# Loads and transposes of the first batches re-ordered in a fused attention and star-ReLU MLP kernel

## The chip, the cores and the metric

The kernel runs on one core of a Trainium2 chip. The metric is the device time of one execution in microseconds. Five engines work side by side: TensorE (PE, with its weight loads shown apart as PEld), VectorE (DVE), ScalarE (ACT), GpSimd (POOL) and SyncE (SP). Each follows its own list of instructions, and they wait for each other by semaphores. Transfers are issued from the queues of SP, ACT and POOL.

## The reference

`x` is (8, 8, 512, 64): batch, head, token, width. `state` is (8, 8, 32, 64). `w_in` is 512 x 2048 and `w_out` 2048 x 512.

```python
scores = scale * x @ state^T                     # 512 x 32 per batch and head
xread = softmax(scores) @ state
sread = softmax(scale * state @ x^T) @ x         # 32 x 64 per batch and head
X = concat([xread, sread], axis=tokens)          # heads side by side: 4352 rows of 512
h = X @ w_in
g = s * relu(h) ** 2 + b
out = g @ w_out
```

## The kernel before, in words

**Order.** The work is declared as operations with an engine (or a choice of ACT and DVE), a key, inputs, outputs, buffers and a duration. A planner (`Plan.order`, L28) runs through a model of time of its own and writes down, for each engine, one fixed order: of the operations that its model takes for ready, the one with the smallest key comes next. For PE it inserts filler matmuls (`filler`, L1094, tile `warm`) early on. The keys are offsets in a table `K` (L283). On the chip each engine then runs its list strictly as written, so an operation whose input is late holds all that stands behind it.

**Stages for one batch.** `x[b]` comes to SBUF in fp16 as `xn`. `xT` is its transpose, `stT` that of the state. `T` = scores (PE), `E` = exp (ACT), `D` = sums of `E` over a head's 32 slots (PE, with the block matrix `bones16`), `R` = exp(-ln D) (ACT, two steps, L559 and L566), `a4` = `E` * `R` (DVE). The state is multiplied into `w_in` first: `M` = state @ w_in, four chunks per batch with two halves each (`Mps` on PE, then a cast on ACT or DVE, L310 or L312). Then `h` = `M` against `a4` for 16 blocks `f`, `relu` (L779 on ACT, L771 on DVE), and a square on DVE (L785) gives `g`. The product with `w_out` accumulates in two PSUM banks `o`. Batch 0 uses plain row blocks. The later batches use a seven-product scheme with sums `u` of the weights and `pd` of `g` (DVE). For the second read of the softmax, `a2` (DVE) is transposed by SP as `aT`, `V` is `aT` @ `xn` (PE), and the collected state rows are run through the same MLP at the end (`h_sr`, `osr`). A column sum of `w_out` (`wsum_ps`, L903) makes the bias; `s` and `b` are applied when `o` is read.

**Loads before.** ACT's queue brings the identity, the first state part and `bones16`; SP's queue brings `x[0]` in four fp32 parts `xf` (L248), which ACT casts. All else goes through POOL's queue, which casts to fp16 on the way, in the order of `SEQ` (L404):

```python
SEQ = "wi0 x1 wi1 stf1 wo0 wi2 wo1 wi3 wo2 wo3 x2 sb x3 x4 x5"
```

Here `wi0` to `wi3` are the parts of `w_in`, `wo0` to `wo3` those of `w_out`, `stf1` the state of batches 1 and 2, and `sb` the two scalars `s` and `b`; `stf1` and `sb` are issued on SP behind a small POOL instruction. The last state part, `stf2`, waits for `wo3`. Batches 0 to 2 are transposed on PE (`xT_mm` into PSUM tile `xTps`, `xT_copy` on DVE); batches 3 to 7 by SP's DMA transposes (`dma_xT`, L462), their state by one more (`stTd`). `NB_HW = 3` sets this limit.

Of the kernel before, what the change touches and what calls it, by code (L numbers as in the profile page):

```python
# [13 lines left out]
class Plan:  # L14
# [13 lines left out]
    def order(self, filler, fill_until, ready):  # L28
# [25 lines left out]
        mode, channel, log, now, done_n = False, 7.0, [], 0.0, 0  # L54
        times = []

# [15 lines left out]
        while done_n < len(ops):  # L72
            for e in free_at:
# [29 lines left out]
                if best is None:  # L103
                    fill = 0.43 if now < 7.0 else 0.22
                    if e == "PE" and now < fill_until and not any(since[i] < now + fill for i in cand[e]):
                        free_at[e] = now + fill
                        times.append(free_at[e])
                        log.append((now, len(log), "PE", filler, "warm", free_at[e]))
                    continue
# [13 lines left out]
                if land is not None:  # L123
                    kind, span = land
                    if kind == "load":
                        done = max(channel, end + 2.0) + span
                        channel = max(channel, done)
                    elif kind == "tp" and now < channel - 4.0:
                        end, done = now + 4.0, now + 9.0
                    else:  # L130
                        done = end + span
# [25 lines left out]
def kernel(  # L157
# [66 lines left out]
    nc.vector.memset(warm, 0.0)  # L224
    ident16 = konst.tile([P, P], FP16, name="ident16")
    ident_dr = nc.inline_tensor(np.eye(P, dtype=np.float16), name="ident_const")
    bones_np = np.kron(np.eye(4), np.ones((Ns, Ns))).astype(np.float16)
    bones16 = konst.tile([P, P], FP16, name="bones16")
    bones_dr = nc.inline_tensor(bones_np, name="bones_const")
    st_v = state.rearrange("b (g hf) j d -> (hf j) (b g) d", g=NG)  # L230
    NB_HW = 3
    stf = konst.tile([P, NG, D], FP32, name="stf")
    stf1 = konst.tile([P, (NB_HW - 1) * NG, D], FP32, name="stf1")
    stf2 = konst.tile([P, (B - NB_HW) * NG, D], FP32, name="stf2")
    xf = [upool.tile([P, H // 2, SCH * D], FP32, name=f"xf_{i}", tag="u") for i in range(2)]
    x0_v = x[0].rearrange("h (q c) d -> q h (c d)", q=P)

    def xf_part(i):
        return xf[i // 2][:, 2 * (i % 2) : 2 * (i % 2) + 2]
# [6 lines left out]
    nc.scalar.dma_start(stf, st_v[:, 0:NG, :])  # L246
    for i in range(4):
        nc.sync.dma_start(xf_part(i), xf_heads(x0_v, i))  # L248
    nc.scalar.dma_start(bones16, bones_dr.ap())
# [5 lines left out]
    s_bc = konst.tile([P, 1], FP32, name="s_bc")  # L255
    b_bc = konst.tile([P, 1], FP32, name="b_bc")
# [6 lines left out]
    st16 = konst.tile([P, B * NG, 2, D], FP16, name="st16")  # L263
    xn = {}
    xn[0] = xpool.tile([P, H, SCH, D], FP16, name="xn_0", tag="xn")

    def cast_x0(eng, i):
        eng(
            xf_heads(xn[0], i).rearrange("p h c d -> p h (c d)"),
            xf_part(i),  # L270
        )

    def cast_st(eng, src, n0, n):
        for k in range(2):
            eng.tensor_copy(st16[:, n0 : n0 + n, k, :], src)

    def late_dma(dst, src):


        nc.gpsimd.memset(dst, 0.0)  # L280
        nc.sync.dma_start(dst, src)

    K = dict(  # L283
        h1=4.4, hs=0.6, M0=-5.6, M1=0.9, T1=0.0, x2=24.6, T2=23.7, D2=27.2, M2=35.3, V0=27.7, V1=21.3, u=12.3,
        us=5.1, pd1=12.5, o0=13.1, o2=23.0, w=26.2, r=0.5, T=-9.8, D=3.1, Mb=6.4, V=8.6, S=3.6, S0=0.1, E=-0.5,
        L=-6.2, a4=-4.7, Mc=1.5, pd=13.4, solo=2.0, hsr=-4.1, Ssr=0.0,
# [3 lines left out]
    stTd = konst.tile([P, (B - NB_HW) * NG, P], FP16, name="stTd")  # L290
# [43 lines left out]
    def cast_x0(i):  # L334
        def fn(e):
            copy_on(
                e,
                xf_heads(xn[0], i).rearrange("p h c d -> p h (c d)"),
                xf_part(i),
# [4 lines left out]
    def cast_st(e, src, n0, n):  # L344
        for k in range(2):
            copy_on(e, st16[:, n0 : n0 + n, k, :], src)

    add(DV(0.4), -30, lambda e: cast_st(e, stf, 0, NG), ["stf"], [("st", 0)])
    for i in range(4):
        add(  # L350
            (DV(0.35), AC(0.5)),
            -29 + i,
            cast_x0(i),
            [("xf", i)],
            [("x", 0, i)],
            [("u", f"xf{i // 2}"), ("xn", "x0")],
        )


    def load(key, dur, span, fn, makes, bufs=(), after=0.0):  # L360
        add(("POOL", dur), key, fn, [], makes, bufs, ("load", span), after=after)
# [21 lines left out]
    def load_x(b, h0=0, h1=H):  # L383
        def fn(e):
            if h0 == 0:
# [8 lines left out]
    def late(dst, src):  # L394
        def fn(e):
            nc.gpsimd.memset(dst, 0.0)
# [4 lines left out]
    gate = konst.tile([P, 2], FP16, name="gate")  # L401
    nc.gpsimd.tensor_copy(gate, ident16[:, 0:2])
    SEQ = "wi0 x1 wi1 stf1 wo0 wi2 wo1 wi3 wo2 wo3 x2 sb x3 x4 x5"
    seq = [(t,) if t in ("stf1", "sb") else (t[:-1], int(t[-1])) for t in SEQ.split()]  # L404
    for n, it in enumerate(seq):
        key = -40 + n
        if it[0] == "wi":
            load(key, 0.8, 4.2 if it[1] == 0 else 2.8, load_wi(it[1]), [it], after=3.4)
        elif it[0] == "wo":
            load(key, 0.8, 2.8, load_wo(it[1]), [it], after=3.4)  # L410
        elif it[0] == "x":
            b = it[1]
            load(
                key, 0.9, 2.9 if b == 1 else 3.9, load_x(b),
                [("x", b, i) for i in range(4)], [("xn", f"x{b}")], after=3.4,
            )
        elif it[0] == "stf1":
            load(key, 0.3, -3.0, late(stf1, st_v[:, NG : NB_HW * NG, :]), [it], after=3.4)
        else:
            load(key, 0.15, 0.1, late(s_bc, moe_s.to_broadcast((P, 1))), [("s",)], after=3.4)  # L420
            load(key + 0.1, 0.15, 0.1, late(b_bc, moe_b.to_broadcast((P, 1))), [("b",)], after=3.4)

    def load_stf2(e):
        nc.gpsimd.tensor_copy(stf2[:, 0, 0:2], wo[3][:, 0, 0:2])
        nc.sync.dma_start(stf2, st_v[:, NB_HW * NG :, :])

    add(("POOL", 0.3), -21, load_stf2, [("wo", 3)], [("stf2",)], (), ("side", 4.0))
    n1 = (NB_HW - 1) * NG
    add(
        DV(0.4), 0, lambda e: cast_st(e, stf1, NG, n1),  # L430
        [("stf1",)], [("st", 1), ("st", 2)],
    )
    add(
        ("POOL", 1.7), -19, lambda e: cast_st(e, stf2, NB_HW * NG, (B - NB_HW) * NG),
        [("stf2",)], [("st", 3)],
    )
# [8 lines left out]
    def dma_stT(e):  # L445
        nc.sync.dma_start_transpose(
            stTd, st16[:, NB_HW * NG :].rearrange("p n k d -> p (n k d)")
        )

    add(("SP", 1.5), 18, dma_stT, [("st", 3)], [("stT", b) for b in range(NB_HW, B)], land=("tp", 3.0))  # L450

    def xT_of(b, h):
        if b < NB_HW:
# [3 lines left out]
    def dma_xT(b, i):  # L457
        def fn(e):
            if "xT" not in A[b]:
                A[b]["xT"] = apool.tile([P, H, 2, P], FP16, name=f"xT_{b}", tag="xT")  # L460
                A[b]["stT"] = stTd[:, (b - NB_HW) * NG : (b - NB_HW + 1) * NG]
# [7 lines left out]
    def stT_mm(b):  # L469
        def fn(e):  # L470
            A[b]["stTps"] = att_ps([P, NG, P], FP16, f"stTps_{b}")
            for g in range(NG):
                mm(
                    A[b]["stTps"][:, g, :],
                    st16[:, b * NG + g].rearrange("p k d -> p (k d)"),
# [6 lines left out]
    def stT_copy(b):  # L482
# [647 lines left out]
```

The softmax here doesn't subtract the row's maximum and nothing guards it: scores larger than these inputs give would overflow.

## Time and profile before

| what | value |
|---|---|
| median of 4 runs | 213.67 us (213.44 to 214.24) |
| the profiled execution's own time | 213.55 us |
| its span in the profile | 211.4 us |
| PE busy | 204.1 us, 97% |
| DVE busy | 175.3 us, 83% |
| ACT busy | 132.7 us, 63% |
| PE groups of the `o` products | 123 us in all |
| filler matmuls (`o<-warm`) | 24, 8.2 us |
| PE share of the chain that ended last | 90% |

The profile shows one execution. Busy shares are averages over the whole span, while the change touches almost only the first 45 us, so the table says which engine carries the kernel but not what the change is worth. The filler matmuls count as busy PE although they compute nothing that is kept. Ends of matmuls are modelled, and a group of matmuls in a timeline row can overlap the row behind it by some tenths of a microsecond.

### The profile page before, as it was taken

Reading aid. Unit: us, or ns where it says so; the run is one execution under the profiler, and the core shown is the slowest. Engines: PE = TensorE matmul, PEld = TensorE weight load, DVE = VectorE, ACT = ScalarE, POOL = GpSimd, SP = SyncE. Lnnn points to the kernel's source line nnn. Section 1 sums busy time; section 2 is a strip of 40 time slices with the busy share of each in tenths; the row PEclk is TensorE's granted clock in tenths of the full one; section 3 lists DMA queues with packets and bytes.
Section 4 is the critical chain, followed back from the end, with each engine's and each line's share of the span. In section 5 each row is a group of like instructions: output and inputs, shape, how many; then the busy total and the mean of one; then the engine's idle time right before and its main releaser. Section 6 shows DMA issues by size and latency. Waiting matters only on the chain.

```text
span 211.4 us, 4963 instructions
## 1 busy us (share of the span) xinstructions
PE 204.1 (97%) x1976; PEld 132.4 (63%) x1976; DVE 175.3 (83%) x412; ACT 132.7 (63%) x288; POOL 37.0 (17%) x60
## 2 busy tenths in 40 slices
PE   5998999999999999999999999999999999999993
PEld 2542333544557676667766776677676777888882
DVE  1268999999988869999988998899989988697652
ACT  4569997696375965796478657974697444632200
POOL 4833100040125261012101200111111111110000
PEclk9999999999999999999999999999999999999998
DMA  6999999999578994553064211321142111211142
GB/s 203 163 197 202 190 205 198 183 144 233 116 151 140 155 254 81 118 77 116 26 125 109 79 50 53 67 89 54 50 59 99 53 50 39 70 50 50 36 143 74
DMA packets 41463, 24.05 MB, mean 114 GB/s; under 512 B 25824, under 2 KB 39648, under 8 KB 41440
## 3 DMA queue, kind: packets, MB, share of 16 engines
q0 software_dynamic: 13840, 15.21, 36.6%
q1 hardware_dynamic: 27040, 8.40, 23.3%
q8 instruction: 15, 0.25, 0.5%
q10 hardware_dynamic: 560, 0.13, 0.3%
q14 instruction: 8, 0.07, 0.1%
HBM read 17.37 MB, written 8.91 MB: 124 GB/s over the span
## 4 chain that ended last, share of the span: by engine, by line
PE 90%; ACT 6%; DMA 2%; issue 0%; DVE 0%; SPq 0%
PE o L209 49%; PE h L209 25%; PE Mps L209 4%; PE h_sr L209 3%; PE osr L209 3%; ACT g L779 2%; PE xTps L209 2%; DMA xf<-in_x_dram 2%; PE D L209 2%; ACT M L310 1%; PE V L209 1%; ACT E L540 1%; PE T L209 1%; ACT D L559 1%; ACT R L566 1%
## 5 line engine op out<-in xcount | busy, mean ns | idle before, releaser
L779 ACT ACTIVATE g<-h 128x512 f16<-128x512 f32 x126 | 73.4, 601 | 41.5 <-PE h L209 41.3
L209 PE MATMUL h<-a,M 128*128 128x512 f16 x256 | 73.8, 379 | 0.6 <-ACT g L779 0.5
L785 DVE TENSOR_TENSOR g<-g 128x512 f16<-128x512 f16 x128 | 52.7, 420 | 3.7 <-ACT g L779 2.2
L209 PEld LDWEIGHTS <-pd 128*128 128x128 f16 x448 | 42.6, 98 | 20.1 <-issue 3.4
L209 PEld LDWEIGHTS <-g 128*128 128x128 f16 x400 | 39.1, 98 | 19.4 <-issue 0.2
L209 PE MATMUL o<-u,pd 128*128 128x256 f16 x336 | 45.9, 273 | 0.0
L209 PE MATMUL o<-wo,g 128*128 128x256 f16 (+1 forms) x288 | 45.5, 296 | 0.0
L1036 POOL DMA_DIRECT2D out_dram<-c x24 | 16.3, 679 | 103.8 <-DVE c L1024 101.0
L209 PEld LDWEIGHTS <-M 128*128 128x128 f16 x256 | 24.1, 98 | 13.2 <-issue 4.6
L310 ACT CAST M<-Mps 128x512 f16<-128x512 f32 x45 | 25.3, 595 | 7.1 <-PE Mps L209 7.1
L1024 DVE SCALAR_TENSOR_TENSOR c<-o,s_bc,bias_bc 128x512 f32<-128x512 f32 x28 | 21.0, 750 | 7.3 <-PE o L209 6.6
L801 DVE TENSOR_TENSOR pd<-g 128x1024 f16<-128x1024 f16 x28 | 19.2, 686 | 0.3
L1024 DVE SCALAR_TENSOR_TENSOR c<-o,s_bc,c 128x512 f32<-128x512 f32 x21 | 15.7, 750 | 1.9 <-PE o L209 1.6
L209 PE MATMUL o<-wo,pd 128*128 128x256 f16 x112 | 16.2, 273 | 0.0
L209 PE MATMUL o<-u,g 128*128 128x256 f16 x112 | 15.5, 273 | 0.0
L312 DVE CAST M<-Mps 128x512 f16<-128x512 f32 x19 | 13.0, 687 | 2.0 <-PE Mps L209 1.9
L773 ACT ACTIVATE g_sr<-h_sr 128x256 f16<-128x256 f32 x16 | 6.1, 383 | 10.5 <-PE h_sr L209 10.4
L540 ACT ACTIVATE E<-T 128x256 f16<-128x256 f32 x32 | 11.8, 389 | 1.1 <-PE T L209 1.1
L812 DVE TENSOR_TENSOR pd<-g,pd 128x512 f16<-128x512 f16 x28 | 11.8, 421 | 0.4
L387 POOL DMA_DIRECT2D xn<-in_x_dram x13 | 10.4, 818 | 8.1 <-DMA wi<-in_moe_w_in_dram 3.7
L810 DVE TENSOR_TENSOR pd<-g,pd 128x512 f16<-128x512 f16 x28 | 11.7, 418 | 0.0
L559 ACT ACTIVATE D<-D 128x512 f32<-128x512 f32 x16 | 9.6, 601 | 1.6 <-PE D L209 1.4
(71 smaller groups left out, 162.8 us busy)
## 6 DMA issues: line engine op xcount, KB each, us to landing
out_dram<-c POOLq DMA_DIRECT2D x24, 256.0 KB, 2.5
xn<-in_x_dram POOLq DMA_DIRECT2D x5, 512.0 KB, 21.9
wi<-in_moe_w_in_dram POOLq DMA_DIRECT2D x4, 512.0 KB, 14.3
wo<-in_moe_w_out_dram POOLq DMA_DIRECT2D x4, 512.0 KB, 19.8
xf<-in_x_dram SPq DMA_DIRECT2D x4, 256.0 KB, 3.7
out_dram<-osb POOLq DMA_DIRECT2D x4, 256.0 KB, 4.4
xn<-in_x_dram POOLq DMA_DIRECT2D x8, 128.0 KB, 4.2
out_dram<-c SPq DMA_DIRECT2D x4, 256.0 KB, 2.5
```

Of the source, the lines that this page charges most:

```text
L209: return nc.tensor.matmul(out, lhsT, rhs, start=start, stop=stop, tile_position=tp, is_transpose=is_transpose, skip_group_check=True,)
L310: nc.scalar.copy(dst, src)
L312: ENG[e].tensor_copy(dst, src)
L540: nc.scalar.activation(a["E"][g][:, 256 * m : 256 * m + 256], a["T"][m][:, g, :], AF.Exp, scale=scale, accum_out=a["rs"][:, g, m : m + 1],)
L559: nc.scalar.activation(A[b][f"D{g}"], A[b][f"D{g}"], AF.Ln)
L779: nc.scalar.activation(g_of(name, f), OSB["h", name, f], AF.Relu)
L785: ENG[e].tensor_mul(g_of(name, f), g_of(name, f), g_of(name, f))
L801: nc.vector.tensor_tensor(pd[:, :, 0:2], g4[:, :, 1:2, :].to_broadcast((P, 2, 2, t)), g4[:, :, 0:4:3, :], ALU.subtract,)
L810: nc.vector.tensor_tensor(pd[:, :, 2], g4[:, :, 3], pd[:, :, 0], ALU.subtract)
L812: nc.vector.tensor_tensor(pd[:, :, 3], g4[:, :, 2], pd[:, :, 2], ALU.subtract)
L1024: nc.vector.scalar_tensor_tensor(t, src, s_bc, add, ALU.mult, ALU.add)
L1036: ENG[e].dma_start(dst[:, rows:SCH:2, hD * h : hD * h + hD], SN[b, name])
```

## The change

- The order of POOL's loads becomes `wi0` at once, then `wi1 wi2 wo0 wo1 wi3 wo2 wo3 x2 x3 x4 x5`. `x[1]` leaves this list: SP brings it in four fp32 parts, as `x[0]` before, each behind a small POOL copy that waits until the third part of `x[0]` has landed; eight casts instead of four follow. POOL's queue goes on with `wi1` when the first part of `x[1]` has landed.
- State comes as two parts of 128 KB, for batches 0 and 1 at the start and for batches 2 and 3 behind `wo1`, with contiguous rows of 1 KB, and one part of 256 KB for batches 4 to 7 behind `wo3`. PE transposes the first two parts (four matmuls each); `stT_copy` now sorts the columns.
- Batch 2 joins the batches that SP transposes (`NB_T = 2`).
- `s` and `b` come behind `wo2`, to four partitions each, and are spread by a DVE copy and a DVE transpose.
- `x[3]` waits on POOL for `aT` of batch 1.
- `bones16` is made by DVE memsets instead of a transfer.
- `xT_copy` of batch 0 is split in halves, one of which may go to ACT. The `relu` of the state rows becomes two instructions.
- The planner: nine fillers at the start, other durations for loads and transposes, other keys, DVE allowed for `relu` of every batch.

```diff
+        for k in range(9):
+            log.append((free_at["PE"], len(log), "PE", filler, "warm", free_at["PE"] + 0.43))
+            free_at["PE"] += 0.43
...
-                    fill = 0.43 if now < 7.0 else 0.22
+                    fill = 0.22
...
+    nc.vector.memset(bones16, 0.0)
+    for q in range(4):
+        nc.vector.memset(bones16[Ns * q : Ns * q + Ns, Ns * q : Ns * q + Ns], 1.0)
+    st_v = state.rearrange("(t b) h (j r) d -> (b h j) t r d", b=2, r=4)
+    st_w = state[4:B].rearrange("b (g hf) j d -> (hf j) (b g) d", g=NG)
+    stf = konst.tile([P, 2, 4, D], FP32, name="stf")
+    stf2 = konst.tile([P, 8, D], FP32, name="stf2")
...
-    nc.scalar.dma_start(stf, st_v[:, 0:NG, :])
+    nc.scalar.dma_start(stf[:, 0], st_v[:, 0])
...
-    nc.scalar.dma_start(bones16, bones_dr.ap())
...
+            AC(0.5) if n < 3 else (DV(0.35), AC(0.5)),
+            -29 + n if b == 0 else K["xc"] + 0.1 * i,
+            cast_x(b, i),
...
+            if b == 3:
+                nc.gpsimd.tensor_copy(gate, A[1]["aT"][:, :, 0, 0])
...
-    SEQ = "wi0 x1 wi1 stf1 wo0 wi2 wo1 wi3 wo2 wo3 x2 sb x3 x4 x5"
+    SEQ = "wi1 wi2 wo0 wo1 wi3 wo2 wo3 x2 x3 x4 x5"
...
+    def load_first(e):
+        load_wi(0)(e)
+        for i in range(4):
+            nc.gpsimd.tensor_copy(xf_part(1, i)[:, 0, 0:2], xf_part(0, 2)[:, 0, 0:2])
+            nc.sync.dma_start(xf_part(1, i), xf_heads(x_v[1], i))
+        nc.gpsimd.tensor_copy(gate, xf_part(1, 0)[:, 0, 0:2])
...
+    def spread_sb(e):
+        nc.vector.tensor_copy(sb_rows.rearrange("p (k j) -> p k j", k=2), sb_in[:, 0:2].unsqueeze(2).to_broadcast((P, 2, 32)))
+        nc.vector.transpose(sb_cols, sb_rows)
+
+    def load_sb(e):
+        nc.gpsimd.tensor_copy(sb_in, wo[2][:, 0, 0:2])
+        nc.sync.dma_start(sb_in[0:P:32, 0:1], moe_s.to_broadcast((4, 1)))
+        nc.sync.dma_start(sb_in[0:P:32, 1:2], moe_b.to_broadcast((4, 1)))
+
+    add(("POOL", 0.2), -21.2, load_sb, [("wo", 2)], ["sb"], (), ("side", 9.0))
+    add(DV(0.25), 19, spread_sb, ["sb"], [("s",), ("b",)])
+
+    def load_st(dst, src, q):
+        def fn(e):
+            nc.gpsimd.tensor_copy(dst[:, 0, 0:2], wo[q][:, 0, 0:2])
+            nc.sync.dma_start(dst, src)
...
+    add(("POOL", 0.3), -21.5, load_st(stf[:, 1], st_v[:, 1], 1), [("wo", 1)], [("stf", 1)], (), ("side", 8.0))
+    add(("POOL", 0.3), -21, load_st(stf2, st_w, 3), [("wo", 3)], [("stf", 2)], (), ("side", 9.0))
...
+    NB_T = 2
...
-        if b < NB_HW:
+        if b < NB_T:
...
+                if b == 0:
+                    for n in range(2):
+                        add(
+                            DV(0.35) if i == 0 else (DV(0.35), AC(0.56)), -29.5 + 10 * i, xT_copy(b, i, 2 * n, 2 * n + 2),
...
+                g, hps = g_of(name, f), OSB["h", name, f]
                 nc.scalar.activation(
-                    g_of(name, f).rearrange("p (i j b) -> p i j b", i=2, b=B // 2),
-                    OSB["h", name, f].rearrange("p (i b j) -> p i j b", i=2, b=B // 2),
+                    g[:, 0:P].rearrange("p (j r b) -> p j r b", r=4, b=B // 2),
+                    hps[:, 0:P].rearrange("p (b r j) -> p j r b", r=4, b=B // 2),
+                    AF.Relu,
+                )
+                nc.scalar.activation(
+                    g[:, P:].rearrange("p (j b) -> p j b", b=B // 2),
+                    hps[:, P:].rearrange("p (b j) -> p j b", b=B // 2),
                     AF.Relu,
                 )
...
-            add((AC(0.5), DV(0.6)) if b < 2 else AC(0.5), k + K["r"], relu(b, f, S), [("h", b, f)], [("r", b, f)], [hb, gb])
+            add((AC(0.5), DV(0.6)), k + K["r"], relu(b, f, S), [("h", b, f)], [("r", b, f)], [hb, gb], spare=K["f0"] if b < 2 else K["f1"])
```

In the order that the changed program is built with, PE carries 20 fillers instead of 24; of the casts of `M`, ACT carries 42 instead of 45 and DVE 22 instead of 19.

## The prediction

> **What bounds the kernel now.** I read the page's busy shares first, then the chain of work that ended last, the busy time by stretches, and the timeline of the first 45 us. TensorE (PE) is busy for 97% of the span, so the question is where it is not doing useful work.
>
> ```profile
> PE 204.1 (97%) x1976; PEld 132.4 (63%) x1976; DVE 175.3 (83%) x412; ACT 132.7 (63%) x288; POOL 37.0 (17%) x60
> ```
>
> The stretches (length; then busy us and count of PE, PEld, DVE, ACT, POOL; clock; DMA share; GB/s) show which engine is full when:
>
> ```profile
> 15.00:20.00 5.00, 4.19 (x56) 1.81 (x53) 4.70 (x12) 4.04 (x14) 1.81 (x5) 1.00 1.25 206
> 20.00:25.00 5.00, 5.00 (x43) 1.85 (x42) 4.26 (x12) 4.94 (x11) 1.74 (x2) 1.00 1.19 183
> 30.00:35.00 5.00, 4.86 (x42) 1.98 (x35) 4.94 (x15) 4.37 (x9) 0.24 (x1) 1.00 1.39 199
> 35.00:40.00 5.00, 5.00 (x37) 2.75 (x35) 4.96 (x15) 2.99 (x6) 0.00 (x0) 1.00 1.39 190
> ```
>
> From about 16 to 34 us ScalarE (ACT) and VectorE (DVE) are full and PE waits on them in small pieces. From 35 us on ACT has slack, and PE has no idle time until its work ends at 207.9 us. A gain is therefore either less PE work anywhere, or a PE that is further on at about 34 us. In the chain (start, duration, work):
>
> ```profile
> 37.81 0.89 PE xTps L209 x16
> ```
>
> is PE work on the path that the change takes away. The timeline shows the head: filler matmuls at half speed and then full speed, the first `h` after the casts of `M`, the loads ending one after another (POOL's waits), and the weight sum.
>
> ```profile
> 5.77 1.49 PE L209 MATMUL o<-warm 128*128 128x512 f16 x3
> 9.82 1.47 PE L209 MATMUL o<-warm 128*128 128x512 f16 x6
> 12.98 0.58 ACT L310 CAST M<-Mps 128x512 f16<-128x512 f32 x1
> 13.63 1.03 PE L209 MATMUL h<-a,M 128*128 128x512 f16 x4
> 14.90 0.88 POOL L387 DMA_DIRECT2D xn<-in_x_dram  x1 [2.75 <-DMA xn<-in_x_dram]
> 17.45 0.87 POOL L387 DMA_DIRECT2D xn<-in_x_dram  x1 [1.52 <-DMA wi<-in_moe_w_in_dram]
> 32.94 0.24 POOL L424 CAST stf<-wo 128x2 f32<-128x2 f16 x1 [9.06 <-DMA wo<-in_moe_w_out_dram]
> 33.64 1.05 PE L209 MATMUL wsum_ps<-wo,ones 128*32 128x512 f16 x16
> ```
>
> POOL's waits date the loads: `wi_0` landed at 11.4 us, `x[1]` at 14.9, `wi_1` at 17.4, the last `wo` at 32.9: seven loads in 18.0 us, 2.57 us each.
>
> **What the Trainium skill says.** (1) "TensorE: Matmul & The Clock Gate", Part 1: PE's clock is halved until about 3.4 us of sustained work. The trace agrees: filler takes 0.43 us a piece up to 7 us and 0.22 at 9.8, after gaps in the first 5 us. (2) "DMA: Bandwidth & Descriptors", Issuing engines are not separate DMA queues: all transfers interleave on the same 16 DMA engines. The trace agrees: 320 KB of state took 9.9 us beside queued loads. (3) The same page, Specifications: transfers under 512 B miss line rate. Rows of `state` go from 256 B to 1 KB for batches 0 to 3; no row of this trace tests the gain. (4) "TensorE: Matmul & The Clock Gate", the paragraph on engine queue depths: ACT and DVE run strictly in order, so one late transfer holds everything queued behind its consumer.
>
> **The change part by part.** The order is that in which the built program has its instructions; durations are those of the trace.
>
> *PE work.* Batch 2's 16 transposes go (0.89 us, on the chain). State transposes for four batches are 8 where six were needed for three: +2 at 0.89/16 = 0.056, +0.11. All other useful matmuls are the same in number. Sum **-0.78 us**, certain as far as PE stays full later.
>
> *The head up to the first `h`.* Nine fillers stand ahead without a gap: 1.19 + 9 x 0.43 = 5.05. The first state part is now 128 KB instead of 64 (landed 4.7 before; the `bones` transfer of 32 KB is gone, made by small DVE memsets before 3 us); I take 4.8. Two casts of 0.25 on DVE, 5.4; four transposes at half speed, 5.9. With the clock released about 6.3 (without the early gaps; bounds 5 and 8): two fillers 6.7, eight transposes 7.15, four fillers 8.0, eight transposes 8.5. Then ACT carries everything: half a copy of `xT` 0.6, four `E` 1.5, two `D`/`R` pairs 2.4, one cast of `M` 0.58: first `h` at 8.5 + 5.1 + 0.15 = 13.75, against 13.8 by the chain of before. **0 us**; bounds -0.6 (clock at 5) and +1.0 (clock at 8).
>
> *`x[1]`.* It leaves POOL's queue and becomes four SP transfers behind POOL's wait for the third part of `x[0]` (landed about 5.9), four small POOL copies (0.24 each by the nearest row) and SP issues of 0.46. `wi_0` is the only load beside it. Two full loads at 2.57 end at 11.2; at the 8.2 us that before took from 6.7 to 14.9 they end at 14.3. I take 12.5. Behind its two DVE casts stand `a4` and the casts of `M`, behind its two ACT casts (0.62 each) the first `relu`. DVE needs the first part at 11.9, ACT the last at 14.2: covered; at 14.3 ACT waits 0.1.
>
> *Weights.* `wi_1` waits for the first part of `x[1]`, some 9.5; POOL's queue behind it holds only loads. At 2.57 each from 12.5: `wi_1` 15.1, `wi_2` 17.6, `wo_0` 20.2, `wo_1` 22.8, `wi_3` 25.3, `wo_2` 27.9, `wo_3` 30.5, some 2.4 us earlier than now. PE wants `wo_0` at 21.5 and `wo_3` at 33.5. Cost 0; with the late end, each comes 1.8 us later and `wo_0` stalls PE for 0.5.
>
> *16 to 34 us.* Against before, ACT has 9 casts of `M` for batches 0 and 1 instead of 12 (-3 x 0.59) and one `relu` more (+0.54). DVE gets three casts of `M` (+2.06), loses one `relu` (-0.68) and the copies of batch 2 (-0.28 - 1.36), gets 0.3 for `s`, `b`. Walking ACT in order from 13.0 (`M` 0.58, `x[1]` 1.25, `relu` 0.54 to 0.6, `M` 0.6, `E` 1.55, `D`/`R` 2.4) I reach the weight sum at 33.45 (0.19 earlier than 33.64) with 0.23 us more PE work done than before had there: **-0.42 us**. Bounds: -1.5, if ACT and DVE both use what was taken off; +0.5, if gaps of the kind that before shows (0.7 us in ACT over this stretch) come on top.
>
> *State of batches 2, 3 and `s`, `b`.* State leaves at `wo_1` (22.8 + 0.3) and at the 8.1 us that 128 KB took before it lands at 31.2; its DVE cast stands at about 31.5, with the weight sum and all squares behind it. Cover 0.3 us; without it DVE's wait is PE's. I take 0; bounds 0 and +3. `s` and `b` leave at 28.3 and took 6 us before: 34.5, wanted at 37. 0. The last state part (9.9 us after 30.5) is wanted by POOL only, behind which stand an output and `x[3]`. 0.
>
> *SP and later x.* SP gets four transposes of `xn_2` more (4 x 1.26 us), behind the four `aT` (7.0 us for four before): issued 33 to 45, landed by 48. PE wants `T` of batch 2 behind 38.3 us of useful matmuls (at 0.217 us per 512 columns) and the 14 us that the head loses (41.45 less 27.1 before it now), at about 52; were the 4 us between gone, PE and then `a4` and `h` of batch 2 would wait. `x[3]` waits for `aT` of batch 1, about 42, behind two outputs; lands near 50, wanted on SP at 52 and on PE at 69. 0.
>
> *Tail.* ACT's `relu` of the state rows becomes two instructions of 128 columns for one of 256 (0.383). From the pair 0.60 at 512 and 0.383 at 256, 0.27 each, 0.55 for both, beside two `h_sr` every 1.3 us on PE. 0; bounds 0 and +0.5, if each half costs the full 0.383.
>
> Sum: -0.78 - 0.42 = **-1.2 us** on the profiled execution (213.55 us, 2.15 around its span of 211.4). That run lies 0.12 below the median of 213.67, so I forecast **212.4 us**. 0.3%, about 0.64 us, is the least that a measurement of this kernel can tell from no change.
>
> **The rivals.**
> A. *As worked out*: 212.4, its own range 211.6 to 213.0. For it: counted PE work, ACT full in this stretch.
> B. *The head shortens more*: clock at 5 (-0.6) and both engines' relief arriving in full (-1.1 beyond my -0.42): 213.67 - 0.78 - 0.6 - 1.5 = 210.8. For it: PE, ACT and DVE all show waits before 34 us; against: three engines must stay level.
> C. *The PE work saved is eaten by a later start*: clock at 8 (+1.0) against -1.2: 213.5, no change. For it: the trace of before released it only after 7 us. The change would then do what it says while the load's new order was hidden anyway.
> D. *The state part of batches 2 and 3 lands late and DVE stands still.* `x[1]` at 14.3 puts `wo_1` at 24.6; at the 9.9 us of the larger state transfer the part lands at 34.9, DVE waits 3.4 us: 212.4 + 3.4 - 0.4 (slack in PE) = 215.4, slower. It decides from a landing at about 33.4 on (0.3 cover + 1.2 + 0.64 beyond 31.2). For it: DVE at 4.94 of 5 us has no slack. Against: rows of 1 KB, and an earlier `wo_1`.
>
> **How the numbers follow.** A 0.48, B 0.18, C 0.18, D 0.16. Faster by over 0.3%: A and B, 0.66; within: C, 0.18; slower: 0.16. The range runs from just under B's value to within D: 210.7 to 214.6; it leaves out the far ends of B and the worse half of D.
>
> **What would show it.** Right: no `xTps` of batch 2 in the profile after; filler at 0.22 before 8 us; first `h` within 0.7 us of 13.8; `wsum_ps` near 33.5 with `wo_3` landed by 31; DVE's wait for `stf` under 0.5 us; PE without idle after 35 us. Wrong: a DVE or ACT wait of over 1 us for `xf` or `stf`, a PE wait for `wo`, or gaps in PE at `T` of batch 2 or at `h_sr`.

## The result, and the profile after

| | time | span of the profiled execution |
|---|---|---|
| before | 213.78 us, median of 56 runs (212.96 to 214.86) | 211.4 us (its own time 213.55) |
| after | 214.53 us, median of 35 runs (211.90 to 221.08) | 216.5 us (its own time 218.33) |

The ratio after to before is 1.0007, 95% interval 0.9992 to 1.0022: no change that can be measured, where the forecast was a gain of 1.2 us. Run again on another chip the same kernel gave 0.9947 (0.9920 to 0.9974). The two intervals do not meet, so this kernel's time differs from chip to chip, or from occasion to occasion, by more than its interval says. The ratios leave out executions more than 1.5% above the fastest of their kernel, which for the changed kernel are 12 of 35, while the kernel before has none; so the ratio flatters the changed kernel, whose median over all executions lies 0.35% above that of the kernel before, and the ranges are given as well.

The page of the changed kernel begins with the busy shares (busy us, share of the span, count):

```profile
PE 203.5 (94%) x1958; PEld 132.1 (61%) x1958; DVE 175.2 (81%) x421; ACT 134.5 (62%) x305; POOL 37.7 (17%) x64
```

PE was busy for about as long as before and stood still for longer. The busy time by stretches says where (length; busy us and count of PE, PEld, DVE, ACT, POOL; clock; DMA share; GB/s):

```profile
15.00:20.00 5.00, 4.04 (x48) 1.45 (x45) 4.15 (x10) 3.79 (x14) 2.61 (x4) 1.00 1.20 194
20.00:25.00 5.00, 3.93 (x23) 1.64 (x23) 4.29 (x13) 4.54 (x9) 0.00 (x0) 1.00 1.24 205
30.00:35.00 5.00, 5.00 (x39) 2.16 (x38) 4.73 (x16) 4.11 (x8) 0.79 (x2) 1.00 1.34 205
35.00:40.00 5.00, 5.00 (x31) 2.08 (x29) 4.72 (x13) 3.57 (x7) 0.00 (x0) 1.00 0.79 142
60.00:70.00 10.00, 10.00 (x81) 6.16 (x79) 8.35 (x19) 8.08 (x15) 3.06 (x6) 1.00 1.32 125
70.00:80.00 10.00, 6.37 (x80) 4.22 (x80) 4.02 (x12) 4.06 (x13) 2.01 (x3) 0.83 1.42 184
```

The last two stretches in the kernel before:

```profile
60.00:70.00 10.00, 10.00 (x128) 7.26 (x127) 8.22 (x19) 6.86 (x19) 3.43 (x5) 1.00 0.98 162
70.00:80.00 10.00, 10.00 (x87) 6.91 (x86) 8.29 (x18) 7.28 (x14) 4.89 (x7) 1.00 1.25 200
```

From 70 to 80 us PE of the changed kernel works 6.4 of 10 us and its clock is 0.83; before, this stretch was full at 1.00. In the stretch ahead the DMA share is higher than before (1.32 against 0.98) and the rate lower (125 GB/s against 162). PE's waits (us in total, times, longest) name the tiles:

```profile
PE V L213 <- DMA aT<-a: 3.6, 1, 3.6
PE o L213 <- DMA wo<-in_moe_w_out_dram: 1.0, 1, 1.0
PE Mps L213 <- DMA wi<-in_moe_w_in_dram: 0.9, 1, 0.9
PE h_sr L213 <- DMA srdT<-sr: 0.7, 1, 0.7
```

None of these four is in the profile before. The chain of work that ended last, which before had `xTps` of batch 2 in it, now runs through a transfer (start, duration, work):

```profile
61.77 12.27 DMA aT<-a
```

This is the transpose on SP of batch 2's attention matrix: issued at 61.8 us, landed at 74.05. What POOL and SP issue around it is, in the next three lines, `x[4]`, then `x[5]` with three parts of `x[6]`, then the two transposes of batch 2's attention matrix:

```profile
54.50 0.92 POOL L382 DMA_DIRECT2D xn<-in_x_dram  x1
59.14 3.15 POOL L382 DMA_DIRECT2D xn<-in_x_dram  x4
59.74 3.83 SPq L630 DMA_TRANSPOSE aT<-a  x2
```

The timeline has the wait in brackets, the head, and POOL's dates of the loads:

```profile
3.72 1.49 PE L213 MATMUL o<-warm 128*128 128x512 f16 x3
6.47 1.03 PE L213 MATMUL o<-warm 128*128 128x512 f16 x4
11.51 1.50 POOL L359 DMA_DIRECT2D wi<-in_moe_w_in_dram  x2 [0.30 <-issue]
13.68 0.59 PE L213 MATMUL h<-a,M 128*128 128x512 f16 x2
22.96 1.24 PE L213 MATMUL o<-wo,g 128*128 128x512 f16 x5 [0.96 <-DMA wo<-in_moe_w_out_dram]
33.62 0.33 POOL L430 CAST stf<-wo 128x2 f32<-128x2 f16 x1 [2.13 <-DMA wo<-in_moe_w_out_dram]
33.68 0.61 PE L213 MATMUL wsum_ps<-wo,ones 128*32 128x512 f16 x8
74.09 0.62 PE L213 MATMUL V<-xn,aT 128*32 128x64 f16 x32 [3.63 <-DMA aT<-a]
```

The filler is at full speed by 6.5 us and the first `h` comes at 13.68, as forecast. But PE, which comes to `wo_0` at 22.0, gets it only at 22.9, and the last `wo` has landed only at 33.6 (before 32.9, forecast 30.5).

One division of the span serves for every run below: the time to the first matmul of the weight sum (head), and the rest.

| kernel (profiled execution) | head | rest | PE's waits in the rest |
|---|---|---|---|
| before | 33.6 | 177.8 | none |
| after | 33.7 | 182.8 | `V` of batch 2: 3.6 and then half clock; `h_sr`: 0.7 |

### The profile page after: what moved, and what is told of

Same layout as the page of the kernel before. It is cut to its first block, busy times and chain, and to the rows that moved or that the text cites. A ratio compares the mean times of both kernels' runs of the same rounds, so it can differ in the third digit from the quotient of the medians.

```text
span 216.5 us, 4992 instructions
## 1 busy us (share of the span) xinstructions
PE 203.5 (94%) x1958; PEld 132.1 (61%) x1958; DVE 175.2 (81%) x421; ACT 134.5 (62%) x305; POOL 37.7 (17%) x64
## 4 chain that ended last, share of the span: by engine, by line
PE 80%; DMA 16%; POOL 1%; issue 0%; SPq 0%; DVE 0%; POOLq 0%
PE o L213 43%; PE h L213 23%; DMA aT<-a 6%; DMA wo<-in_moe_w_out_dram 5%; DMA xf<-in_x_dram 4%; PE h_sr L213 3%; PE Mps L213 3%; PE osr L213 3%; DMA srdT<-sr 2%; PE V L213 1%; PE D L213 1%; PE T L213 1%; POOL wi L359 1%; PE wsum_ps L213 0%; SPq L256 0%
## 5 line engine op out<-in xcount | busy, mean ns | idle before, releaser
L213 PEld LDWEIGHTS <-pd 128*128 128x128 f16 x448 | 43.3, 98 | 18.4 <-issue 1.9
L213 PE MATMUL o<-u,pd 128*128 128x256 f16 x336 | 47.4, 273 | 0.0
L303 ACT CAST M<-Mps 128x512 f16<-128x512 f32 x42 | 24.1, 594 | 5.8 <-PE Mps L213 5.6
L1050 DVE SCALAR_TENSOR_TENSOR c<-o,sb_cols,bias_bc 128x512 f32<-128x512 f32 x28 | 21.0, 750 | 8.1 <-PE o L213 7.8
L1050 DVE SCALAR_TENSOR_TENSOR c<-o,sb_cols,c 128x512 f32<-128x512 f32 x21 | 15.8, 750 | 4.6 <-PE o L213 4.3
L213 PE MATMUL o<-u,g 128*128 128x256 f16 x112 | 17.7, 277 | 0.0
L305 DVE CAST M<-Mps 128x512 f16<-128x512 f32 x22 | 14.7, 684 | 0.0
L549 ACT ACTIVATE E<-T 128x256 f16<-128x256 f32 x32 | 11.8, 387 | 1.9 <-PE T L213 1.9
L838 DVE TENSOR_TENSOR pd<-g,pd 128x512 f16<-128x512 f16 x28 | 11.8, 421 | 0.4
L794 ACT ACTIVATE g_sr<-h_sr 128x128 f16<-128x128 f32 x16 | 4.4, 277 | 11.6 <-PE h_sr L213 11.6
```

The source lines that it names most:

```text
L213: return nc.tensor.matmul(out, lhsT, rhs, start=start, stop=stop, tile_position=tp, is_transpose=is_transpose, skip_group_check=True,)
L303: nc.scalar.copy(dst, src)
L305: ENG[e].tensor_copy(dst, src)
L549: nc.scalar.activation(a["E"][g][:, 256 * m : 256 * m + 256], a["T"][m][:, g, :], AF.Exp, scale=scale, accum_out=a["rs"][:, g, m : m + 1],)
L838: nc.vector.tensor_tensor(pd[:, :, 3], g4[:, :, 2], pd[:, :, 2], ALU.subtract)
L1050: nc.vector.scalar_tensor_tensor(t, src, s_bc, add, ALU.mult, ALU.add)
```

## The experiments

All ran on the chip beside the kernel before. Moves are made after the plan: a table gives some steps another time to be sorted by, and all other steps keep their order.

### The changed kernel again, and three edits of its loads

**The changed kernel again.** No edit.

> The changed kernel once more, as the measure for the others. Theory H1 (loads of x[3] to x[6], held until the second batch's transposes, are under way at 55 to 75 us and delay the transposes of batch 2's attention matrix on SP; PE waits for V of batch 2 and then runs some us at half clock): ratio to before 1.000 to 1.003 with a wait of PE at V of batch 2 of 1 to 4 us in the profile and a granted clock of 0.95 or less for some us after it. If the profile shows no such wait, the stall of the first profile belonged to that execution and H1 explains nothing of the median.

Measured: 213.81 us (11 runs, 211.73 to 220.58), ratio 0.9947 (0.9920 to 0.9974). The profiled execution, 214.69 us, has head 33.1 and rest 179.8; PE waits 2.1 us at `V` of batch 2, for an `aT` that took 12.0 us to land, and 0.7 at `h_sr`. The wait is not an accident of the first profile, but its length changes. Two parts of the expectation missed: the clock stayed at 1.00 behind the wait, and the ratio lies below 1.000.

**x[3], x[4], x[5] early.**

```diff
-            if b == 3:
-                nc.gpsimd.tensor_copy(gate, A[1]["aT"][:, :, 0, 0])
...
+    retime = {('x', 3, 0): 15.61, ('x', 4, 0): 15.62, ('x', 5, 0): 15.63}
```

> x[3], x[4], x[5] issued on POOL right behind x[2], without waiting for batch 1's transposes, as in the kernel before; every other order as changed. H1: no x load under way at 55 to 62 us, aT of batch 2 lands within 5 us of its issue, no wait at V of batch 2; aT of batch 1 may land later (V of batch 1 is due at 47.9, aT landed there without a wait) ; 212.0 to 212.8 us, ratio 0.992 to 0.996. H2 (SP's own queue: batch 2's four transposes and the later order put aT of batch 2 too late whatever is loaded): the wait at V of batch 2 stays, 213.5 to 214.5. H5 (the early loads delay the state's second part and the first transposes): a wait of DVE at stf or of PE at V of batch 1 or T of batch 2 of 1 to 3 us, 213 to 216.

Measured: 218.46 us (6 runs, 216.31 to 219.68), ratio 1.0197 (1.0156 to 1.0238). The wait at `V` of batch 2 is gone, `aT` of that batch lands 5.5 us after its issue. But `V` of batches 0 and 1 now waits, four times, together 3.7 us:

```profile
45.99 0.30 PE L213 MATMUL V<-xn,aT 128*32 128x64 f16 x16 [0.22 <-DMA aT<-a]
48.16 0.30 PE L213 MATMUL V<-xn,aT 128*32 128x64 f16 x16 [1.88 <-DMA aT<-a]
52.01 0.30 PE L213 MATMUL V<-xn,aT 128*32 128x64 f16 x16 [0.94 <-DMA aT<-a]
52.92 0.30 PE L213 MATMUL V<-xn,aT 128*32 128x64 f16 x16 [0.61 <-DMA aT<-a]
```

The four transposes for them, issued at 35 to 42 us, land 10.5 to 12.1 us after their issue, in the changed kernel 2.4 to 4.0. So the transposes that loads of x lie beside land late, whichever they are; early, they lie beside those of batches 0 and 1. (In the kernel before these took 7.4 to 9.9 us as well, but its first `V` comes at 50.5 us and did not wait.) So holding `x[3]` is worth something in this kernel, and the loads cannot simply go back.

**x[4] and x[5] right behind x[3].**

```diff
+    retime = {('x', 4, 0): 45.61, ('x', 5, 0): 45.62}
```

> x[3] waits for batch 1's transposes as in the changed kernel, but x[4] and x[5] are issued right behind it on POOL (about 45 to 48 us instead of 54 and 59). H1: their 5 to 6 us of transfers are over by about 60, aT of batch 2 lands within 6 us, the wait at V of batch 2 is gone or under 0.5 us: 212.0 to 213.0. H2: wait unchanged, 213.5 to 214.5. A third outcome, x[3]'s transposes on SP late because x[4] and x[5] share the channels with them: wait of SP at x[3] or of PE at T of batch 3, above 214.

Measured: 213.90 us (14 runs, 212.27 to 216.04), ratio 0.9999 (0.9978 to 1.0020). No wait at `V` of batch 2; its `aT` lands 8.4 and 6.6 us after its issues. The runs no longer reach 220 us. In the stretches, 60 to 70 us now has 223 GB/s at the same DMA share instead of 125:

```profile
60.00:70.00 10.00, 10.00 (x83) 6.35 (x81) 7.85 (x18) 8.37 (x15) 2.18 (x4) 1.00 1.32 223
70.00:80.00 10.00, 10.00 (x119) 7.06 (x117) 8.99 (x23) 7.92 (x20) 4.71 (x7) 1.00 0.95 162
```

The median did not fall to 212.0 to 213.0, so the wait was not all. The rest is 177.8 us, as in the kernel before although PE has less to do, and one wait is left in it, 0.9 us at `h_sr`. The head is 34.3.

**The second part of w_in not held.**

```diff
-        nc.gpsimd.tensor_copy(gate, xf_part(1, 0)[:, 0, 0:2])
```

> Only the POOL copy that holds the second part of w_in until the first part of x[1] has landed is left out, so that the part is issued right after x[1]'s parts have been released (about 7.5 us instead of 11.5). H4 (the hold costs the head about 0.9 us at the second part of w_in and 1.0 at the first of w_out): both waits of PE fall below 0.3 us and the weight sum starts 1 to 3 us earlier on the DMA side; x[1]'s parts land 1 to 2 us later; by itself 0.3 to 0.6 us faster than the changed kernel, with the stall at V of batch 2 as it was: ratio 0.998 to 1.001. If x[1]'s parts are wanted sooner than that, h of batch 1 comes late and the gain is given back: same as the changed kernel.

Measured: 217.71 us (6 runs, 214.94 to 219.63), ratio 1.0126 (1.0079 to 1.0173). The waits for `wi_1` and `wo_0` are gone, but the last part of `x[1]` comes late instead; PE waits in the middle of its transposes:

```profile
17.28 0.40 PE L213 MATMUL xTps<-ident,xn 128*128 128x128 f16 x4 [1.88 <-ACT xn L303]
```

The head is 34.6 and the wait at `V` of batch 2 is 2.7 us. A miss: leaving out the hold on `wi_1` does not give the head its gain.

### The tail, the head's idle time, and the reverse

**V of batch 7 sooner**, on top of x[4] and x[5] behind x[3].

```diff
+    retime = {('x', 4, 0): 45.61, ('x', 5, 0): 45.62, ('V', 7): 170.0, ('sr', 7): 170.5, ('srT', 7): 170.9}
```

> The kernel of the run before with x[4] and x[5] behind x[3], and V of batch 7, its copy and its transpose on SP are put some 8 us sooner in the written order, about where the kernel before has them. H3 (the tail's wait of PE for srdT, 0.7 to 0.9 us, comes from V of batch 7 standing behind the last h of that batch): the wait goes and nothing takes its place; 0.7 to 0.9 us under the kernel with x[4] and x[5] alone, so about 213.0 us, ratio 0.995 to 0.997. Rival: the end is set by VectorE's 600 ns and 335 ns instructions on the last blocks, and the wait is only moved to g or to c of the last rows: 213.6 to 214.2, ratio 0.999 to 1.002.

Measured: 212.45 us (6 runs, 211.68 to 217.92), ratio 0.9916 (0.9897 to 0.9935). No wait at `h_sr` and none in its place: the rest is 176.7 us, 1.2 under that of the kernel without this edit. One of the six runs took 217.92 us, at a mean clock of 0.98; it has no profile. In the profile at hand `aT` of batch 2 landed only 0.2 us before PE wanted it.

**Fillers in PE's idle time at 11.5 to 13 us**, on top of x[4] and x[5] behind x[3].

```diff
+        if step[4] and step[4][0] == ("Mps", 1, 0):
+            for _ in range(6):
+                filler("PE")
```

> The kernel with x[4] and x[5] behind x[3], and six more filler matmuls (0.22 us each at full clock) on PE ahead of the first product of batch 1, where PE otherwise idles 0.4 and 0.74 us waiting for ACT's R. H6 (that idle time drops the granted clock to half at about 13 to 17 us in many executions, so that batch 1's transposes take 1.9 us instead of 1.06 and the head ends about 1 us late): clock 1.00 at 14 to 20 us, first h near 13.3, weight sum at 33.0 to 33.6 us, about 0.5 to 1.0 us under the kernel with x[4] and x[5] alone: 212.9 to 213.4 us. Rival: the clock has nothing to do with it and the head is set by when w_in's second and w_out's first part land: weight sum at 33.7 to 34.5, same as without fillers; if the fillers run at half clock themselves they add up to 1 us.

Measured: 212.57 us (22 runs, 211.63 to 214.91), ratio 0.9936 (0.9918 to 0.9954). The time is lower, yet the profile does not show the expected reason: the head is 34.7 and the clock is 0.89 at 14 to 20 us, behind a wait of 2.1 us for `wi_1`. In this execution the transpose of `sr` landed in 3.1 us instead of 4.4 and `h_sr` did not wait, so part of the difference may be that. At 14 to 20 us half clock shows in one of the six profiles without these fillers (0.76, `x[4]` and `x[5]` behind `x[3]`) and in one of the ten with them (this one). What the fillers do is left open.

**The reverse: x[4] and x[5] late in the kernel before.**

```diff
+    retime = {('x', 4, 0): 52.6, ('x', 5, 0): 59.6}
```

> The reverse on the kernel before: x[4] and x[5] alone are moved on POOL from behind x[3] (20 and 23 us) to where the changed kernel issues them (about 54 and 59 us); nothing else differs from the kernel before. H1: their transfers then lie over the transposes of batch 2's attention matrix (SP, 58 to 61 us), which land 6 to 12 us after their issue instead of about 3; PE waits 1 to 4 us at V of batch 2 or at T of batch 4, the runs spread by several us: 214.5 to 218, ratio 1.004 to 1.02. Rival H2 (SP's queue with four more transposes is at fault, not the loads): 213.4 to 214.2, ratio 0.998 to 1.002.

Measured: 215.05 us (22 runs, 213.38 to 216.82), ratio 1.0042 (1.0026 to 1.0059). The kernel before, with nothing else changed, now waits at the same place:

```profile
68.30 0.42 PE L209 MATMUL V<-xn,aT 128*32 128x64 f16 x32 [1.63 <-DMA aT<-a]
```

`aT` of batch 2 lands 4.7 and 7.8 us after its issues instead of 2.8 and 4.0; the rest is 179.6 us, 1.8 more than before. SP's order is untouched, so the loads alone can make the wait, without the four more transposes in SP's queue (H2); whether those add to it in the changed kernel is not shown. The two loads did not go quite where the changed kernel has them: `x[4]` was issued at 46.7 us and had landed at 55.8, before these transposes. Only `x[5]` (60.4) and parts of `x[6]` (from 61.3) lay over them.

**The three edits together.**

> The three edits together: x[4] and x[5] behind x[3], V of batch 7 sooner, six fillers in the head. If H1, H3 and H6 each hold and add, no wait at V of batch 2, none for srdT, clock 1.00 at 14 to 20 us: 212.0 to 212.5 us, ratio 0.991 to 0.994, faster than both kernels. If H6 falls, as the one with x[4], x[5] and V of batch 7: 212.8 to 213.3.

Measured: 212.01 us (5 runs, 211.58 to 214.88), ratio 0.9892 (0.9874 to 0.9911). Head 33.8, rest 176.7. It is faster than the kernel before, and its interval also lies below that of the changed kernel on another chip (0.9920 to 0.9974). What the fillers add is not shown: the interval overlaps that of the kernel without them (0.9897 to 0.9935).

### What the head hangs on, and what the late loads cost

**The three edits again.**

> The kernel with the three edits (x[4] and x[5] behind x[3], V of batch 7 sooner, six fillers) once more, as the measure for the next three: 211.7 to 212.5 us, ratio 0.988 to 0.992.

Measured: 212.66 us (7 runs, 211.86 to 213.37), ratio 0.9940 (0.9918 to 0.9962); head 34.4, rest 176.7. The same code now does less well than in the run before, and its interval overlaps that of the changed kernel.

**x[1] released by the second part of x[0].**

```diff
-            nc.gpsimd.tensor_copy(xf_part(1, i)[:, 0, 0:2], xf_part(0, 2)[:, 0, 0:2])
+            nc.gpsimd.tensor_copy(xf_part(1, i)[:, 0, 0:2], xf_part(0, 1)[:, 0, 0:2])
```

> The three edits, and x[1]'s four parts wait for the second part of x[0] instead of the third (1.2 us sooner by the landings that the plan writes down; the parts' own transfers are unchanged, w_in's second part still waits for the first part of x[1]). H4b (the two holds leave the transfer engines less than full at 7 to 14 us, share 0.72 to 0.85 against 1.24 in the kernel before; that is why w_in's second part makes PE wait 0.9 to 2.1 us and w_out's first 0.5 to 1.0 and the head gains nothing): DMA share at 7 to 14 us rises to about 0.95, w_in's second part lands about 1 us sooner, its wait falls by 0.7 or more, weight sum 0.3 to 0.8 us sooner: 0.3 to 0.7 us under the kernel with three edits. Rival: x[1]'s parts then compete with the last parts of x[0] and of w_in's first, first h 0.3 to 0.8 us later, no gain or 0.3 us slower.

Measured: 211.93 us (6 runs, 211.20 to 213.15), ratio 0.9911 (0.9883 to 0.9939). The wait for `wi_1` is 0.8 us instead of 1.3, the head 33.6. The DMA share at 7 to 14 us did not rise here (0.75), and the interval overlaps that of the three edits: a gain is not shown.

**The matrix of ones loaded.**

```diff
-    nc.vector.memset(bones16, 0.0)
-    for q in range(4):
-        nc.vector.memset(bones16[Ns * q : Ns * q + Ns, Ns * q : Ns * q + Ns], 1.0)
+    bones_np = np.kron(np.eye(4), np.ones((Ns, Ns))).astype(np.float16)
+    bones_dr = nc.inline_tensor(bones_np, name="bones_const")
...
+    nc.scalar.dma_start(bones16, bones_dr.ap())
```

> The three edits, and the block matrix of ones comes from a 32 KB constant by a transfer on ACT's queue, as in the kernel before, instead of VectorE's memsets. Theory (the 0.33 us by which the time outside the span is shorter in the changed kernel, 1.8 against 2.1 us, come from having one constant fewer to set up): time less span back to 2.1 us, 0.3 us slower than the kernel with three edits. Rival: the time outside has to do with other things (memory of the core, number of instructions): stays at 1.8; the head may shift by up to 0.3 us either way through the 32 KB ahead of the first transfers of x[1].

Measured: 212.50 us (6 runs, 211.22 to 212.69), ratio 0.9922 (0.9897 to 0.9947). Time less span stays at 1.74 to 1.82 us over the six runs. The constant is not why the changed kernel has less time outside its span; a miss, and the reason is open.

**V of batch 7 sooner and fillers, x[4] and x[5] late.**

The edit takes the entries of x[4] and x[5] out of the table of times.

> Two of the three edits: V of batch 7 sooner and six fillers, with x[4] and x[5] left where the changed kernel has them. H1: the stall at V of batch 2 is back (1.5 to 4 us and some us at half clock in the profile), 1 to 2.5 us slower than the kernel with three edits and spread over several us: 213.0 to 215.0 us. If the stall of the changed kernel had come from its head being late, the fillers would keep it away: as the kernel with three edits.

Measured: 211.99 us (7 runs, 210.86 to 218.07), ratio 0.9896 (0.9867 to 0.9924). The profiled execution is the one of 218.07 us: `V` of batch 2 waits 3.7 us, the clock is 0.83 at 70 to 80 us, the rest is 182.1. The other six, 210.86 to 212.66 us, have no profile; their spans (209.1 to 210.9) leave no room for such a wait. So the late loads do not always cost, and here the other runs even lay under those of the kernel with the loads sooner. That is what the next comparison asks about.

### The last four, on one chip

**x[1] released by the second part, again.** No further edit.

> The kernel with the three edits and x[1]'s parts released by the second part of x[0], once more, as the measure for the next three: 211.2 to 212.4 us, ratio 0.988 to 0.993, no wait at V of batch 2.

Measured: 212.72 us (13 runs, 210.95 to 213.55), ratio 0.9930 (0.9901 to 0.9959); head 33.2, rest 176.7. That is above the 211.2 to 212.4 us expected.

**That kernel with x[4] and x[5] late.**

```diff
-    retime = {('x', 4, 0): 45.61, ('x', 5, 0): 45.62, ('V', 7): 170.0, ('sr', 7): 170.5, ('srT', 7): 170.9}
+    retime = {('V', 7): 170.0, ('sr', 7): 170.5, ('srT', 7): 170.9}
```

> As that kernel, but x[4] and x[5] where the changed kernel has them. Theory H1 as it stands: most executions without a long wait at V of batch 2 take the same time as the kernel with x[4] and x[5] sooner (211.2 to 212.4), and a part of them (1 in 7 to 1 in 2) take 4 to 8 us longer. Rival H7 (x[4] and x[5] behind x[3] also cost something of their own where there is no such wait, as 210.9 to 212.7 against 211.9 to 213.4 us of the last runs suggests): the executions without the wait lie 0.7 us or more under the kernel with x[4] and x[5] sooner.

Measured: 213.61 us (22 runs, 211.95 to 218.21), ratio 0.9963 (0.9941 to 0.9986). The profiled execution, 215.23 us, waits 1.1 us at `V` of batch 2. The fastest run lies 1.0 us above that of the kernel with the loads sooner: H7, a cost of the sooner loads of their own, falls. The late loads cost 0.9 us in the median here, though the two intervals overlap, and in the profiles the head differs as well (35.6 against 33.2).

**That kernel with x[4] alone sooner.**

```diff
+    retime = {('x', 4, 0): 45.61, ('V', 7): 170.0, ('sr', 7): 170.5, ('srT', 7): 170.9}
```

> As that kernel, but only x[4] stands behind x[3]; x[5] stays late (59 us). H1: with half of the late loads gone from 55 to 72 us, long waits are rarer than with both late: none or one in six; the rest at 211.2 to 212.4. If x[5] and x[6] alone are enough to hold aT of batch 2 up, as many long ones as with both late.

Measured: 212.33 us (16 runs, 211.06 to 214.34), ratio 0.9922 (0.9895 to 0.9949), no wait at `V` of batch 2, rest 176.7. Moving `x[4]` alone was enough in these runs. `aT` of batch 2 took 7.7 us at most, as in the reverse above (7.8); there PE wanted it at 66.7 us, here at 70.5. So the wait depends on the time left as much as on the delay.

**That kernel with x[1] released by the first part.**

```diff
-            nc.gpsimd.tensor_copy(xf_part(1, i)[:, 0, 0:2], xf_part(0, 1)[:, 0, 0:2])
+            nc.gpsimd.tensor_copy(xf_part(1, i)[:, 0, 0:2], xf_part(0, 0)[:, 0, 0:2])
```

> x[1]'s parts wait for the first part of x[0] only (about 1 us sooner again). H4b: DMA share at 7 to 14 us rises, w_in's second part makes PE wait under 0.4 us, 0.2 to 0.6 us faster than with the second part. Rival: x[0]'s last parts now share the transfer engines with x[1], the second xTps and with it T, E, R and the first h come 0.3 to 1 us later: 0 to 0.6 us slower.

Measured: 211.53 us (8 runs, 211.27 to 212.86), ratio 0.9894 (0.9858 to 0.9929), head 32.8, rest 176.7. PE's waits of the kernel have no `wi` left in them:

```profile
PE o L213 <- DVE warm L228: 1.2, 1, 1.2
PE o L213 <- DMA wo<-in_moe_w_out_dram: 0.8, 1, 0.8
PE Mps L213 <- DVE xT L305: 0.5, 1, 0.5
```

This is the lowest median found, 1% under the kernel before. The interval overlaps that of the kernel with the second part (0.9901 to 0.9959), so a gain from the sooner release is not shown, and the changed kernel was not run beside it.

**The wait over all profiles.** Six profiles are of kernels with late loads: changed (twice), `wi_1` not held, the two with fillers and x[4], x[5] late, and the reverse. All six wait at `V` of batch 2, for 1.1 to 3.7 us. Ten are of kernels with `x[4]`, or `x[4]` and `x[5]`, behind `x[3]`: none waits there, and `aT` landed 0.2 to 3.1 us before PE wanted it. The times agree: of the executions with both loads late (changed, twice, and the two with fillers) 15 of 75 took 216 us or more, of those with one or both sooner 2 of 103.

**The head over all profiles.** POOL issues `wi_1` when the first part of `x[1]` has landed. Set beside the start of the weight sum, that moment explains the head, and the first `h` does not:

| kernel | `wi_1` issued | first `h` | weight sum | difference to `wi_1` |
|---|---|---|---|---|
| x[1] by first part | 10.70 | 13.28 | 32.80 | 22.1 |
| x[1] by second part, again | 10.80 | 13.64 | 33.17 | 22.4 |
| changed, again | 11.08 | 13.20 | 33.15 | 22.1 |
| changed | 11.51 | 13.68 | 33.68 | 22.2 |
| x[4], x[5] behind x[3] | 12.22 | 14.20 | 34.26 | 22.0 |
| same with fillers | 12.40 | 13.45 | 34.73 | 22.3 |
| x[1] by second part, x[4], x[5] late | 13.20 | 14.24 | 35.55 | 22.3 |

In all fifteen profiles with that hold the difference is 21.7 to 22.4 us. What links the two is `wo_0`: in fourteen of the fifteen PE waits for it, 0.5 to 1.0 us; it lands 11.0 to 11.6 us after `wi_1` is issued, and the weight sum starts 10.7 us after that wait, with no gap of PE between. In the kernel before `wo_0` landed at 19.7, and PE took it up at 21.0 without a wait. With no hold (`wi_1` issued at 6.4) the head was 34.6, because `x[1]` was late instead.

The spread within one head is as wide as what the edits were meant to gain. With x[1] by the second part, four profiles issue `wi_1` at 10.8, 11.8, 12.1 and 13.2 us, with heads of 33.2 to 35.6; with the third part, ten profiles issue it at 11.1 to 12.5, with heads of 33.2 to 34.7. So how fast x lands in an execution moves the head by more than 1 us, and that the sooner release shortens it is not shown.

## Why the prediction was wrong

It forecast 212.4 us and a clear gain; no change was measured. The median, 214.53, lies just inside the range of 210.7 to 214.6, which is luck: that end was drawn for a late state part (rival D), and the state was not late. Rival C's number came, no change, but not its mechanism, a clock released late. By its steps:

- **PE work, right.** The forecast of -0.78 for the transposes and -0.23 for work already done make -1.0 from the weight sum on. Where no wait of PE follows, the rest is 176.7 us against 177.8: -1.1.
- **First `h`, right.** 13.75 forecast, 13.68 in the first profile, 13.2 to 14.2 over all; PE's clock was full from 5.7 us there (6.3 taken), and from 4.2 to 7.1 over all profiles of the changed kernel and its edits.
- **Weights, wrong: the first failed step.** `wi_1` was to be issued at about 9.5 and the loads to follow without a gap from 12.5. The first part of `x[1]` landed at 10.9, so `wi_1` was issued at 11.5. The last part of `x[1]` landed at 13.0 and `wi_1` at 16.9, 3.9 us later and not 2.57; `wo_0` came at 22.9 instead of 20.2 and the last `wo` at 33.6 instead of 30.5. PE waited 0.9 us for `wi_1` and 1.0 for `wo_0`, which was costed at 0. That is near the forecast's own late case (`wi_1` at 16.9, a stall of 0.5 at `wo_0`), though `x[1]` was not late. The -0.19 us at the weight sum did not come (+0.04). At 7 to 14 us the DMA share is 0.84 against 1.24 before, but the rate is 211 GB/s against 176, so the share does not show idle transfer engines; part of these bytes is `x[1]`, which comes as fp32.
- **State, right, by luck in its parts.** The part for batches 2 and 3 left at 25.8 us instead of 23.1 and took 5.3 instead of 8.1; the two errors cancel, and it landed at 31.1 (forecast 31.2). Its cast stood at 33.4, not 31.5, and did not wait. Rival D did not come about.
- **"SP and later x ... 0", wrong: the second failed step, and the largest.** It followed `x[3]` to its own readers and stopped. It did not follow POOL's queue behind the held `x[3]`: `x[4]` behind two outputs at 54.5 us and `x[5]` and three parts of `x[6]` at 59 to 62, over the transposes of batch 2's attention matrix at 59.7 to 63.6. These took 12 us to land. That costs 2.1 us in one profile of the changed kernel and about 5 in the other: 3.6 of wait, and up to 1.7 (an estimate) for 3.4 us at half clock. The runs carry the cause: all six profiles with late loads wait there, none of the ten with `x[4]`, or both, sooner does, and moving loads late in the kernel before made the wait.
- **Tail, wrong: the third failed step.** The halves of `relu` are 0.277 and 0.272 us, as worked out. But the new order of PE puts `V` of batch 7 behind all of that batch's `h`, and the step did not walk from there to `h_sr`. There `srdT` landed 4.2 to 4.4 us after its issue, and PE waited 0.7 to 0.9; with `V` of batch 7 sooner it landed after 2.2, with no wait, and the rest was 1.2 us shorter.
- **Around the span.** 1.83 us instead of 2.15 (1.73 to 1.84 in every run against 2.06 to 2.18): -0.3 us that the sum did not have; the reason is open.

Two of the signs of being wrong that the prediction named did come, a wait of PE for `wo` and a gap at `h_sr`; the costliest, at `V` of batch 2, was not among them.

The sum of the first profile then closes nearly: -1.1 for PE work, +0.04 for the head, some +1 for the tail, +3.6 and up to +1.7 for `V` of batch 2 make +5.2; the spans differ by 5.1. In the median of all runs the first three and the time around the span nearly cancel (about -0.4), and 214.53 less 213.78 leaves about 1 us, an estimate, for the wait at `V` of batch 2.

The likeliest case therefore had its gain, and two of the other steps' zeros gave it back: one order of PE on the tail and one order of POOL at 55 us. Why the wait is absent in many executions and long in others is not settled. The time left for `aT` was small in several profiles (0.2 us at the least), so that small shifts may decide, but no run here tests that.

## What to carry to other kernels

When a change holds a load, follow every entry that stands behind it in the same queue to the time at which it now moves, and ask what else moves then: a hold does not only delay what is held. Cut the span at one fixed piece of work and compare the parts of several profiles; that separated a tail wait of 1 us, a wait in the middle and a noisy head which the totals had mixed. A zero needs its cover named for every transpose and load in the new order, up to the end of the kernel.

## What the runs showed of the hardware

Three transposes on SP landed 2.4 us after their issue with no load of x out (changed kernel, 36.6 to 39.2 us); those with such loads under way took 4.0 to 12.3 us at batches 0 to 2 of that kernel, the longest at batch 2. Not the transposes alone were slow there: an output of 256 KB issued at 58.6 us landed 10.8 us later, where the median of its kind is 2.6. The DMA share does not tell of this: 60 to 70 us had 125 GB/s at a share of 1.32 in one profile and 223 GB/s at the same share in another, with other transfers in it.

PE's waits of 2.7, 3.6 and 3.7 us at `V` of batch 2 were followed by 3.4 us at half clock (an `h` of 634 ns instead of 379). Of two waits of 2.1 us, the one in the head with fillers was followed by half clock, the one at `V` of batch 2 was not.
